# The last 64 tokens of one attention parity laid behind the other, so that two short last units become one full unit

## The chip, the cores and the metric

The kernel runs on one core of a Trainium2 chip. The metric is the device time of one execution in microseconds (us). A time is quoted as the median of several executions. One profiled execution of each kernel gives its trace: the span from first to last event, and for each engine the instructions with start, duration and the event that released them.

Short names in the profile: PE is TensorE (matmuls), PEld its weight loads, DVE is VectorE, ACT is ScalarE, POOL is GpSimd, SP is SyncE, which only issues transfers here. A trailing q (SPq, POOLq) is the engine's instruction sequencer. L562 is line 562 of the kernel file. Matmul lines have other numbers before and after the change, because the file grew.

The runs compared below are in the fast state, with a granted clock (the share of TensorE's full clock that the profile reports) of 0.99 to 1.00.

## The reference, cut to what matters

```python
x = A_x                                    # 1 x 2048 x 512
xn = _layernorm(x)
s = A(xn, wqkv, wo)                        # sliding, dilated attention
g = _silu(B(xn, w1, w2, w3, w4))           # mixer MLP with token shifts
return x + s * g

# A: 32 heads of 16; a token looks at itself and at 7 earlier tokens, 2 apart
W, dil = 8, 2
idx = pos[:, None] - arange(W)[None, :] * dil
logits = where(idx >= 0, q . k[idx] * Dh ** -0.5, -1e9)
o = softmax(logits) . v[idx];  A = o @ wo

# B
h  = gelu(_layernorm(x) @ w1);  hs = shifted quarters of h @ w2
x1 = x + hs
B  = x1 + gelu(_layernorm(x1) @ w3) @ w4
```

The dilation of 2 means that even tokens see only even tokens and odd tokens only odd ones. The kernel therefore works on two parities of M = 1024 tokens each. Inside a parity the window is 8 adjacent tokens.

## The kernel before

A parity is cut into units of queries. A unit of nq queries needs nq + 8 keys, so 120 queries fill the 128 partitions with keys. The first unit has 128 queries (no halo). 1024 = 128 + 7 x 120 + 56, so each parity ends in a short unit of 56 queries:

```python
NQ, M = 120, S // 2
units = [(0, P, 0, P)]                     # (first query, queries, first key, keys)
while units[-1][0] + units[-1][1] < M:
    q0 = units[-1][0] + units[-1][1]
    nq = min(NQ, M - q0)
    units.append((q0, nq, q0 - W, nq + W))
NU = len(units)                            # 9, the last one short
```

Each unit costs the same number of instructions, whatever its length:

```python
def values(p, u):                          # 4 matmuls of 512 columns      (L542)
    ...
    for dt in range(ND):
        nc.tensor.matmul(vp[:nk, :], lhsT=xnT[p][:, dt, k0 : k0 + nk], rhs=wv_sb[:, dt, :], ...)

def scores(p, u, dd):                      # twice per unit: 16 matmuls of nq columns (L562), 2 exps (L567)
    ...
            nc.tensor.matmul(st[:nk, b, i * nq : (i + 1) * nq],
                             lhsT=kT[e][r : r + 32, dt, k0 : k0 + nk],
                             rhs=qT[e][r : r + 32, dt, q0 : q0 + nq], ...)
        nc.scalar.activation(prv[:nk, 2 * h : 2 * h + 2], st[:nk, :, 0 : 4 * nq], AF.Exp, scale=SCALE)

def weighted(p, u, va, prs):               # 32 matmuls of nq columns      (L585)
    ...
```

Between the two score halves of a unit the kernel places matmuls of other work, so that TensorE has something to do while ScalarE computes the exps. In parity 0 this filler is the remaining q/k projections ("q", 4 matmuls, L414) and the w2 tiles ("w", 4 matmuls, L452):

```python
for n, (a, b) in enumerate((("www", "qq"), ("q", "wq"), ("q", "wq"), ("q", "ww"), ("q", "ww"),
                            ("q", "ww"), ("q", "ww"), ("q", "ww"), ("q", "w"))):
    # a: filler after the first score half, b: after the second
```

In parity 1 it is the w4 tiles (11 matmuls each, L516). Between the parities lies w3 (176 matmuls, L496) without attention. After parity 1 come eight more w4 tiles, and beside them the final tiles: attention output times wo (L672), times the gate (VectorE, L680), plus x (VectorE, L682), and the store of the result.

```python
weighted(*prev)()
...
for i in (0, 2, 4):
    store(nc.sync, 0, i)                   # 2 row tiles each
for t in range(8, 16):
    w4s[t](0, NF)
    ...                                    # one final tile beside each w4 tile
```

All long-lived data lies in one large "arena" at fixed offsets; a region is used again when its first owner is done.

The softmax here doesn't subtract the row's maximum and nothing guards it: scores larger than these inputs give would overflow.

## Time and profile before

| | before |
|---|---|
| time, median of 3 runs | 209.36 us (209.29 to 209.38) |
| span of the profiled execution | 207.58 us |
| TensorE busy | 198.6 us, 96% |
| VectorE, ScalarE, GpSimd busy | 66%, 65%, 36% |
| head: start to the first scores of parity 0 | 45.99 us |
| parity 0: to the first w3 matmul | 45.92 us |
| w3: to the first scores of parity 1 | 38.51 us |
| parity 1: to the last weighted sum | 44.39 us |
| last weighted sum to the end of the last w4 matmul | 25.57 us |

From the page of the kernel before: the busy table (engine, busy us, share of the span, number of instructions) and the chain that ended last, by engine.

```profile
PE 198.6 (96%) x1990; PEld 97.0 (47%) x2019; DVE 137.2 (66%) x269; ACT 133.9 (65%) x162; POOL 75.3 (36%) x146
PE 75%; DVE 11%; POOL 6%; issue 3%; ACT 3%; DMA 1%
```

TensorE is the bound.

The end of parity 0 in the TensorE timeline of before (start us, duration us, engine, line, operation, operands, shapes, count):

```profile
...
87.98 0.50 PE L562 MATMUL s_ps<-arena 32*64 32x56 bf16 x16
...
89.82 1.03 PE L542 MATMUL v_ps<-wv_sb,arena 128*128 128x512 bf16 x4
90.77 0.33 PE L562 MATMUL s_ps<-arena 32*64 32x56 bf16 x16
...
91.91 1.89 PE L496 MATMUL w_ps<-arena 128*128 128x512 bf16 x8
93.73 0.39 PE L585 MATMUL o_ps<-arena,v_aug 64*32 64x56 bf16 x32
...
```

The two lines with 32x56 are the scores of the short unit of parity 0. The line L585 with 64x56 is its weighted sum; it is already inside w3, because a weighted sum is always issued behind the next unit's first scores. The last matmul of a group is drawn out to its modelled end, so the cost of a group is best read as the distance to the start of the next one: 16 short scores cost 0.26 to 0.43 us, 32 short weighted matmuls 0.33 us.

The end of parity 1 in the same view:

```profile
...
171.13 0.33 PE L562 MATMUL s_ps<-arena 32*64 32x56 bf16 x16
...
173.36 0.33 PE L562 MATMUL s_ps<-arena 32*64 32x56 bf16 x16
...
174.81 0.39 PE L585 MATMUL o_ps<-arena,v_aug 64*32 64x56 bf16 x32
175.36 2.32 PE L516 MATMUL w_ps<-arena 128*128 128x512 bf16 x10 [0.16 <-issue]
```

```profile
174.36 0.39 PE L585 MATMUL o_ps<-arena,v_aug 64*32 64x56 bf16 x32
174.68 2.55 PE L516 MATMUL w_ps<-arena 128*128 128x512 bf16 x11
```

The stages by windows of time. Columns: window, its length, then busy time and instruction count of PE, PEld, DVE, ACT and POOL, the granted clock, DMA share and GB/s.

```profile
45.99:91.91 45.92, 45.16 (x684) 22.23 (x693) 33.40 (x58) 38.51 (x50) 23.08 (x48) 1.00 0.58 124
91.91:130.42 38.51, 38.30 (x205) 17.74 (x208) 13.68 (x31) 23.16 (x25) 6.85 (x13) 1.00 0.74 164
130.42:174.81 44.39, 43.92 (x680) 21.30 (x688) 30.60 (x39) 37.03 (x46) 15.74 (x22) 1.00 0.42 95
174.81:200.38 25.57, 25.30 (x147) 11.70 (x150) 21.10 (x35) 5.04 (x8) 4.03 (x8) 1.00 0.37 104
```

In each of the four stages TensorE is busy all but a small part, and no other engine comes near it except ScalarE in the two attention stages (38.5 and 37.0 us).

### The profile page before, as it was taken

The numbers are of one execution on the slowest core, as the hardware profiler recorded it, in microseconds if no ns is written. First come the engines' busy times: TensorE is split into PE (matmuls) and PEld (weight loads), VectorE is DVE, ScalarE is ACT, GpSimd is POOL, SyncE is SP. The second block draws the span as 40 slices with busy tenths as digits, with TensorE's granted clock in tenths as the row PEclk, the third lists the DMA queues.
The fourth block names the chain that finished last, engine by engine and source line by source line (L and its number), as shares of the span: only waits on it lengthen the run. The fifth ranks groups of instructions, "written<-read, shape, count | busy, mean of one in ns | idle before, by whom it ended". The sixth has DMA issues, their size and how long they took to land.

```text
span 207.6 us, 4987 instructions
## 1 busy us (share of the span) xinstructions
PE 198.6 (96%) x1990; PEld 97.0 (47%) x2019; DVE 137.2 (66%) x269; ACT 133.9 (65%) x162; POOL 75.3 (36%) x146
## 2 busy tenths in 40 slices
PE   7899999999999999999999999999999999999991
PEld 2565455444544445454444444444445444444440
DVE  4789988645387888787860100268666959779794
ACT  2374878868988888775556555898889875122120
POOL 6788544300032869940164000000850392700000
PEclk9999999999999999999999999999999999999999
DMA  5992066046810576786358994779040042455202
GB/s 145 351 348 71 7 101 96 1 71 101 257 52 0 141 158 107 154 190 113 106 118 216 169 313 92 106 162 305 6 86 3 13 109 42 97 151 156 75 32 101
DMA packets 30575, 25.56 MB, mean 123 GB/s; under 512 B 12488, under 2 KB 28200, under 8 KB 30552
## 3 DMA queue, kind: packets, MB, share of 16 engines
q1 hardware_dynamic: 28360, 21.96, 42.9%
q0 software_dynamic: 2048, 3.15, 9.0%
q8 instruction: 16, 0.26, 0.6%
q10 hardware_dynamic: 144, 0.13, 0.2%
q14 instruction: 7, 0.06, 0.1%
HBM read 12.39 MB, written 4.46 MB: 81 GB/s over the span
## 4 chain that ended last, share of the span: by engine, by line
PE 75%; DVE 11%; POOL 6%; issue 3%; ACT 3%; DMA 1%
PE w_ps L516 19%; PE w_ps L496 18%; PE v_ps L542 8%; PE w_ps L452 7%; PE s_ps L562 6%; PE wo_ps L672 6%; PE o_ps L585 4%; PE qk_ps L414 4%; POOL l1r L273 3%; PE w_ps L429 3%; DVE l1s L280 2%; ACT arena L567 2%; DVE arena L327 1%; DVE l0s L303 1%; DMA arena<-in_A_x_dram 1%
## 5 line engine op out<-in xcount | busy, mean ns | idle before, releaser
L567 ACT ACTIVATE arena<-s_ps 128x960 bf16<-128x960 f32 (+2 forms) x72 | 63.0, 928 | 13.7 <-PE s_ps L562 13.4
L516 PE MATMUL w_ps<-arena 128*128 128x512 bf16 (+1 forms) x156 | 38.5, 380 | 0.5 <-issue 0.2
L501 ACT ACTIVATE arena<-w_ps 128x1024 bf16<-128x1024 f32 x20 | 20.5, 1023 | 15.3 <-PE w_ps L496 14.6
L627 POOL DMA_DIRECT2D arena<-orw x48 | 25.0, 527 | 8.7 <-DVE orw L597 7.4
L496 PEld LDWEIGHTS <-arena 128*128 128x128 bf16 (+1 forms) x176 | 17.6, 100 | 20.2
L516 PEld LDWEIGHTS <-arena 128*128 128x128 bf16 (+1 forms) x176 | 16.4, 98 | 19.6 <-issue 0.4
L546 DVE CAST v_aug<-v_ps 128x512 bf16<-128x512 f32 (+1 forms) x18 | 12.4, 689 | 19.5 <-PE v_ps L542 19.5
L682 POOL TENSOR_TENSOR arena<-arena 128x512 bf16<-128x512 bf16 x6 | 7.7, 1302 | 45.0 <-DVE arena L680 45.0
L531 ACT ACTIVATE sig<-arena 128x512 bf16<-128x512 bf16 x16 | 10.1, 630 | 21.4 <-DVE arena L522 21.4
L597 DVE CAST orw<-o_ps 128x960 bf16<-128x960 f32 (+2 forms) x18 | 19.7, 1094 | 2.1 <-PE o_ps L585 2.1
L496 PE MATMUL w_ps<-arena 128*128 128x512 bf16 (+1 forms) x86 | 19.4, 379 | 0.1
L398 PE MATMUL qk_ps<-arena 128*128 128x512 bf16 (+1 forms) x102 | 18.6, 329 | 0.8 <-ACT arena L320 0.5
L496 PE MATMUL w_ps<-arena,arena 128*128 128x512 bf16 (+1 forms) x86 | 19.1, 379 | 0.1
L542 PE MATMUL v_ps<-wv_sb,arena 128*128 128x512 bf16 (+1 forms) x71 | 18.5, 380 | 0.1
L562 PEld LDWEIGHTS <-arena 32*128 32x128 bf16 (+1 forms) x576 | 10.8, 94 | 15.6 <-issue 15.5
L562 PE MATMUL s_ps<-arena 32*128 32x120 bf16 (+2 forms) x576 | 16.8, 211 | 0.1
L272 POOL TENSOR_SCALAR l3r<-l3m 128x1 f32<-128x1 f32 (+1 forms) x10 | 2.3, 226 | 38.5 <-DVE l3m L281 38.5
L522 DVE TENSOR_TENSOR arena<-w_ps,arena 128x512 bf16<-128x512 f32 x16 | 11.1, 692 | 7.8 <-PE w_ps L516 7.7
L653 DVE TENSOR_TENSOR arena<-arena,orw 128x1440 bf16<-128x1440 bf16 (+1 forms) x2 | 1.7, 842 | 21.3 <-DMA orw<-rden_d 21.3
L452 PE MATMUL w_ps<-arena 128*128 128x512 bf16 x63 | 15.2, 380 | 0.2 <-issue 0.2
L429 PE MATMUL w_ps<-arena 128*128 128x512 bf16 x62 | 14.4, 379 | 0.1
L398 PEld LDWEIGHTS <-arena 128*128 128x128 bf16 x104 | 10.0, 98 | 7.5 <-DMA arena<-in_A_wqkv_dram 0.6
(101 smaller groups left out, 283.9 us busy)
## 6 DMA issues: line engine op xcount, KB each, us to landing
arena<-arena SPq DMA_DIRECT2D x48, 64.0 KB, 2.5
x1n_dram<-arena SPq DMA_DIRECT2D x4, 512.0 KB, 3.4
arena<-in_A_x_dram SPq DMA_DIRECT2D x4, 512.0 KB, 5.2
out_dram<-arena SPq DMA_DIRECT2D x7, 256.0 KB, 2.1
arena<-in_A_x_dram SPq DMA_DIRECT2D x6, 256.0 KB, 7.1
arena<-in_B_w_dram SPq DMA_DIRECT2D x1, 1376.0 KB
arena<-in_B_w_dram SPq DMA_DIRECT2D x1, 1280.0 KB
arena<-in_A_wqkv_dram SPq DMA_DIRECT2D x2, 512.0 KB, 4.5
```

The costliest lines, as they stand in the source:

```text
L398: nc.tensor.matmul(pt[:, b, hh * w : (hh + 1) * w], lhsT=wqk_sb[:, dt, nt * P : (nt + 1) * P], rhs=xnT[p][:, dt, k * CH + hh * w : k * CH ...
L429: nc.tensor.matmul(pt[:, b, :], lhsT=w1_sb[:, dt, g * P : (g + 1) * P], rhs=xn2T[c][:, dt, :], start=(dt == 0), stop=(dt == ND - 1),)
L452: nc.tensor.matmul(pt, lhsT=w2_src(p, g, m0), rhs=w2_sb[:, g, :], start=(g == 0), stop=(g == ND - 1))
L496: nc.tensor.matmul(pt[:fs, ft % 2, :], lhsT=w3_sb[:, dt, ft * P : ft * P + fs], rhs=x1nT[c][:, dt, :], start=(dt == 0), stop=(dt == ND - 1),)
L501: nc.scalar.activation(h3(c, 2 * a, 2), pt, AF.Gelu_apprx_tanh)
L516: nc.tensor.matmul(pt, lhsT=h3(c, ft, 1)[:fs, 0, jj * P : (jj + 1) * P], rhs=w4_sb[:fs, ft, :], start=(ft == 0), stop=(ft == NF - 1),)
L542: nc.tensor.matmul(vp[:nk, :], lhsT=xnT[p][:, dt, k0 : k0 + nk], rhs=wv_sb[:, dt, :], start=(dt == 0), stop=(dt == ND - 1),)
L562: nc.tensor.matmul(st[:nk, b, i * nq : (i + 1) * nq], lhsT=kT[e][r : r + 32, dt, k0 : k0 + nk], rhs=qT[e][r : r + 32, dt, q0 : q0 + nq], s ...
L567: nc.scalar.activation(prv[:nk, 2 * h : 2 * h + 2], st[:nk, :, 0 : 4 * nq], AF.Exp, scale=SCALE)
L597: nc.vector.tensor_copy(out=orw[p][:, :, :, q0 - ra : q0 - ra + nq], in_=op[:, :, 0 : 4 * nq].rearrange("p j (s q) -> p j s q", q=nq),)
L627: nc.gpsimd.dma_start(out=oT[p][DH * hh : DH * (hh + 1), :, ra : ra + rw], in_=orw[p][32 * cg : 32 * cg + DH, jj],)
L672: nc.tensor.matmul(pt, lhsT=oT[p][:, dt, i * P : (i + 1) * P], rhs=wo_sb[:, dt, :], start=(dt == 0), stop=(dt == ND - 1),)
```

## The change

The intent: do not pay for two short units. Parity 0 gets 8 units and stops 56 tokens early. Its last 64 tokens, of which the first 8 are the halo, are laid into columns 1024 to 1087 behind parity 1. Then parity 1's last unit has 56 + 64 = 120 queries, a full unit. (The 8 halo columns also run as queries; their results are thrown away.) The number of units falls from 18 to 17.

The extra columns have to be filled for q, k, the mask rows and the transposed input, and the results of the 56 tokens must come back to parity 0. Because each lengthened buffer of q, k and the transposed input needs 0.5 KB more per partition, the arena map was redone. One ring of buffers went from 3 to 2. And the same filler tiles had to be spread over 8 units of parity 0, not 9. The diff, cut to its core:

```diff
+    DW = 64
     units = [(0, P, 0, P)]
     while units[-1][0] + units[-1][1] < M:
         q0 = units[-1][0] + units[-1][1]
-        nq = min(NQ, M - q0)
-        units.append((q0, nq, q0 - W, nq + W))
+        units.append((q0, NQ, q0 - W, NQ + W))
     NU = len(units)
+    N1 = NU - 1
+    order = [(0, u) for u in range(N1)] + [(1, u) for u in range(NU)]
...
-    fin = ctx.enter_context(tc.tile_pool(name="fin", bufs=3))
+    fin = ctx.enter_context(tc.tile_pool(name="fin", bufs=2))
...
+    X = M + DW
-    arenas = [... enumerate((164, 16))]               # KB
+    arenas = [... enumerate((166 * KB + 160, 16 * KB))]
... (all offsets of the arena map)
 def mask_fill(k):
+                if k:
+                    nc.vector.tensor_copy(out=(kT, qT)[w][e][:, :, M:X], in_=mask[:, w, DW : 2 * DW]...)
...
+    def stage_x():
+        nc.gpsimd.tensor_copy(out=xnT[1][:, :, M:X], in_=xnT[0][:, :, M - DW : M])
...
 def qk_pair(c, a, halves=1):
                 nc.scalar.copy(out=dst[:, n0 : n0 + 2, k * CH : (k + 1) * CH], in_=pt)
+                if c == 1:
+                    nc.scalar.copy(out=dst[:, n0 : n0 + 2, M:X], in_=pt[:, :, CH - DW : CH])
...
 def normalise_end(p, r):          # the columns past M go to parity 0's output
+        if rw > n:
+            a = M - DW + W
+            nc.vector.tensor_tensor(out=oT[0][:, :, a:M], in0=oT[p][:, :, a + DW : X], ...)
...
-        (("www", "qq"), ("q", "wq"), ("q", "wq"), ("q", "ww"), ("q", "ww"), ("q", "ww"), ("q", "ww"), ("q", "ww"), ("q", "w"))
+        (("www", "qq"), ("q", "ww"), ("qw", "qw"), ("q", "ww"), ("qw", "qw"), ("q", "ww"), ("qw", "qw"), ("q", "w"))
...
-                load_w4()
-                load_wo()
+            if c == 1 and a == 0:
+                load_wo()
+                load_w4()
...
+    w4s[8](0, 4)                  # 4 matmuls before the last weighted sum
     weighted(*prev)()
...
-    fq = [(0, 6), (0, 7)] + [(1, i) for i in range(8)]
+    fq = [(0, 6)] + [(1, i) for i in range(6)]
     for t in range(8, 16):
-        w4s[t](0, NF)
+        w4s[t](4 * (t == 8), NF)
...
-    final_tile(1, 5, ps=psa)
-    store(nc.sync, 1, 4)
+    final_tile(0, 7, ps=psa)      # needs the last unit now, so it moved to the end
+    store(nc.sync, 0, 7, 1)
```

The two row tiles (0, 6) and (0, 7) were stored together before; now they end far apart and are stored one by one.

More of the change, by code (lines that the diff above doesn't have):

```diff
@@ L54 @@
         q0 = units[-1][0] + units[-1][1]
-        nq = min(NQ, M - q0)
-        units.append((q0, nq, q0 - W, nq + W))
+        units.append((q0, NQ, q0 - W, NQ + W))
     NU = len(units)
+    N1 = NU - 1
+    order = [(0, u) for u in range(N1)] + [(1, u) for u in range(NU)]
     runs = []
-    for cuts in ((0, 3, 6, NU), (0, 3, 6, NU)):
+    for cuts in ((0, 3, 6, N1), (0, 3, 6, NU)):
         runs.append(
@@ L78 @@
     KB = 512
-    arenas = [const.tile([P, n * KB], BF16, name=f"arena{i}") for i, n in enumerate((164, 16))]
+    X = M + DW
+    arenas = [const.tile([P, n], BF16, name=f"arena{i}") for i, n in enumerate((166 * KB + 160, 16 * KB))]
     def at(kb, n, m):
-        ar, o = (arenas[0], int(kb * KB)) if kb < 164 else (arenas[1], int((kb - 176) * KB))
+        ar, o = (arenas[0], int(kb * KB)) if kb < 170 else (arenas[1], int((kb - 176) * KB))
         return ar[:, o : o + n * m].rearrange("p (n m) -> p n m", n=n)
@@ L85 @@
     xn = [at(8 * p, M // P, D) for p in range(2)]
-    kT = [at(16 + 8 * e, ND, M) for e in range(2)]
-    qT = [at(32 + 8 * e, ND, M) for e in range(2)]
-    kq = [[at(48 + 16 * p + 8 * w, ND, M) for w in range(2)] for p in range(2)]
-    mask = at(152, 2, M)
-    wide = at(157, 2, M)
-    xnT = [at(80 + 8 * p, ND, M) for p in range(2)]
-    hT = [at(96 + 8.5 * p, ND, M + 2) for p in range(2)]
-    wqk_sb = at(113, ND, 2 * D)
-    w1_sb = at(121, ND, D)
-    w2_sb = at(125, ND, D)
-    xn2T = [at(129 + 4 * (c % 2), ND, CH) for c in range(NCH)]
@@ L97 @@
-    w3_sb = at(137, ND, F)
-    prob = [at(148 + 4 * i, 1, H * P // 2) for i in range(4)]
-    orws = [const.tile([P, 2 * ND * RW], BF16, name=f"orw{i}") for i in range(2)]
-    oT = [at(176, ND, M), at(129, ND, M)]
-    xn3 = at(129, TPC, D)
-    x1nT = [at(a, ND, CH) for a in (133, 188, 184, 148)]
-    h3T = [at(a, NF, CH) for a in (48, 96, 107)]
-    h3T_lo, h3T_hi = at(80, 8, CH), at(188, NF - 8, CH)
-    w4_sb = at(118, NF, D)
-    wo_sb = at(59, ND, D)
-    xo = [at(137, M // P, D), at(64, M // P, D)]
@@ L108 @@
-    rr_at = (184, 72)
+    kT = [at(16 + 8.5 * e, ND, X) for e in range(2)]
+    qT = [at(33 + 8.5 * e, ND, X) for e in range(2)]
+    kq = [[at(50 + 8.5 * w, ND, X) for w in range(2)], [at(67 + 8 * w, ND, M) for w in range(2)]]
+    xnT = [at(83, ND, M), at(91, ND, X)]
+    hT = [at(99.5 + 8.03125 * p, ND, M + 2) for p in range(2)]
+    B0 = 115.5625
+    wqk_sb = at(B0, ND, 2 * D)
+    w1_sb = at(B0 + 8, ND, D)
+    w2_sb = at(B0 + 12, ND, D)
+    xn2T = [at(B0 + 16 + 4 * (c % 2), ND, CH) for c in range(NCH)]
@@ new lines @@
+    w3_sb = at(B0 + 24, ND, F)
+    Q0 = B0 + 24 + 10.75
+    prob = [at(Q0 + 4 * i, 1, H * P // 2) for i in range(4)]
+    mask = at(Q0 + 4, 2, M)
+    wide = at(Q0 + 9, 2, M)
+    orws = [const.tile([P, 2 * ND * RW], BF16, name=f"orw{i}") for i in range(2)]
+    oT = [at(176, ND, M), at(B0 + 17, ND, X)]
+    xn3 = at(B0 + 17, TPC, D)
+    x1nT = [at(a, ND, CH) for a in (62, 188, 184, Q0)]
+    h3T = [at(a, NF, CH) for a in (50, 99.5, 110.5)]
+    h3T_lo, h3T_hi = at(83, 8, CH), at(188, NF - 8, CH)
@@ L110 @@
+    w4_sb = at(121.5, NF, D)
+    wo_sb = at(62, ND, D)
+    xo = [at(B0 + 25.5, M // P, D), at(67, M // P, D)]
+    rr_at = (184, 75)
+    sg_at = (61, 66, B0 + 33.5)
     cnt = {"v": 0, "p": 2, "b": 0, "r": 0, "g": 0}
@@ L169 @@
     warm(10)
-    tab = at(148, 3, P + 24)
+    tab = at(Q0, 3, P + 24)
     mg = small.tile([P, 4], F32, name="mg", tag="mg", bufs=1)
@@ L246, in mask_fill @@
                 )
+                if k:
+                    nc.vector.tensor_copy(
+                        out=(kT, qT)[w][e][:, :, M:X],
+                        in_=mask[:, w, DW : 2 * DW].unsqueeze(1).to_broadcast([P, ND, DW]),
+                    )
     def spread(p, lo, hi, q=nc.sync, ws=(0, 1)):
@@ L365, in stage_d @@
         r2 = r2s.pop(c)
-        dg = at(156, TPC, P)
+        dg = at(Q0 + 8, TPC, P)
         for j in range(TPC):
@@ L577, in weighted @@
             rw = runs[p][r][3]
-            orw[p] = orws[(3 * p + r) % 2][:, 0 : 2 * ND * rw].rearrange("p (j s q) -> p j s q", j=2, s=ND)
+            orw[p, r] = orws[(3 * p + r) % 2][:, 0 : 2 * ND * rw].rearrange("p (j s q) -> p j s q", j=2, s=ND)
         op = pst("o", "o_ps")
@@ L597, in weighted_out @@
         nc.vector.tensor_copy(
-            out=orw[p][:, :, :, q0 - ra : q0 - ra + nq],
+            out=orw[p, r][:, :, :, q0 - ra : q0 - ra + nq],
             in_=op[:, :, 0 : 4 * nq].rearrange("p j (s q) -> p j s q", q=nq),
@@ L611, in normalise @@
             out=den_d.rearrange("(j c) x -> c j x", j=2),
-            in_=orw[p][DH : P : 32].rearrange("c j s q -> c j (s q)"),
+            in_=orw[p, r][DH : P : 32].rearrange("c j s q -> c j (s q)"),
         )
@@ L628, in pack @@
                     out=oT[p][DH * hh : DH * (hh + 1), :, ra : ra + rw],
-                    in_=orw[p][32 * cg : 32 * cg + DH, jj],
+                    in_=orw[p, r][32 * cg : 32 * cg + DH, jj],
                 )
@@ L646, in normalise_rr @@
         else:
-            rr = at(rr_at[r % 2] if p else 121, 1, ND * rw)[:, 0, :]
+            rr = at(rr_at[r % 2] if p else B0 + 8, 1, ND * rw)[:, 0, :]
         nc.sync.dma_start(out=rr, in_=rden_d.unsqueeze(1).to_broadcast([8, DH, ND * rw]))
@@ L652, in normalise_end @@
         _, _, ra, rw = runs[p][r]
+        rr = rrs[p, r].rearrange("p (s q) -> p s q", s=ND)
+        n = min(rw, M - ra)
         nc.vector.tensor_tensor(
-            out=oT[p][:, :, ra : ra + rw], in0=oT[p][:, :, ra : ra + rw],
-            in1=rrs[p, r].rearrange("p (s q) -> p s q", s=ND), op=ALU.mult,
-        )
+            out=oT[p][:, :, ra : ra + n], in0=oT[p][:, :, ra : ra + n], in1=rr[:, :, 0:n], op=ALU.mult
+        )
+        if rw > n:
+            a = M - DW + W
+            nc.vector.tensor_tensor(
+                out=oT[0][:, :, a:M], in0=oT[p][:, :, a + DW : X], in1=rr[:, :, a + DW - ra : rw], op=ALU.mult
+            )
     def load_wo():
@@ L676, in final_tile @@
         cnt["g"] += 1
-        sg = at(75 + cnt["g"] % 4, 1, D)[:, 0, :]
+        sg = at(sg_at[cnt["g"] % 3], 1, D)[:, 0, :]
         if act:
@@ L748 @@
         qk_pair(1, a)[0]()
+    stage_x()
     stage_t(2, 0)
@@ L767 @@
     mask_fill(1)
-    spread(0, CH, M)
+    spread(0, CH, X)
     stage_w1(2, 1)
@@ L773 @@
     va = values(0, 0)
-    N1 = NU
-    order = [(p, u) for p in range(2) for u in range(NU)]
-    groups = {n: ([], []) for n in range(2 * NU)}
+    groups = {n: ([], []) for n in range(len(order))}
     def w2_and(t):
@@ L791 @@
     assert not w2q and not qkq
-    late = {n: [] for n in range(2 * NU + 4)}
+    late = {n: [] for n in range(len(order) + 4)}
     def st3(n, *ts):
@@ L800 @@
     late[3] += [lambda: ln3_norm(0), lambda: normalise_dn(0, 0), lambda: ln3_turn(0)]
-    st3(4, 4, 5)
-    st3(5, 6)
-    st3(6, 7)
-    late[7] += [lambda: ln3_norm(1), lambda: normalise_dn(0, 1), lambda: ln3_turn(1)]
+    st3(3, 4)
+    st3(4, 5, 6, 7)
+    late[6] += [lambda: ln3_norm(1), lambda: normalise_dn(0, 1), lambda: ln3_turn(1)]
     w4s = [w4_tile(t) for t in range(S // P)]
@@ L828 @@
             b.append(lambda i=i2: final_tile(0, i, nc.gpsimd))
-    for p in range(2):
-        for r, (_, end, _, _) in enumerate(runs[p]):
-            n = p * NU + end
-            if n + 1 < 2 * NU and not (p == 0 and n >= N1):
-                late[n].append(lambda p=p, r=r: pack(p, r))
-                if p:
-                    late[n].append(lambda p=p, r=r: normalise_dn(p, r))
-                if n < 6 or n > N1:
-                    late[n + 2].append(lambda p=p, r=r: normalise_mid(p, r))
-                    late[n + 2].append(lambda p=p, r=r: normalise_rr(p, r))
-                if p and r == 0:
-                    late[n + 4].append(lambda p=p, r=r: normalise_end(p, r))
-    CUT = CH
+    for n, p, r in ((3, 0, 0), (6, 0, 1), (N1 + 3, 1, 0), (N1 + 6, 1, 1)):
+        if (p, r) != (0, 1):
+            late[n].append(lambda p=p, r=r: pack(p, r))
+        if p:
+            late[n].append(lambda p=p, r=r: normalise_dn(p, r))
+        if (p, r) != (0, 1):
+            late[n + 2].append(lambda p=p, r=r: normalise_mid(p, r))
+            late[n + 2].append(lambda p=p, r=r: normalise_rr(p, r))
+    late[N1 + 7].append(lambda: normalise_end(1, 0))
+    CUT = 480
     for w in range(2):
-        late[4 + w].append(lambda w=w: spread(1, 0, CUT, nc.gpsimd, (w,)))
+        late[3 + w].append(lambda w=w: spread(1, 0, CUT, nc.gpsimd, (w,)))
     prev = None
@@ L882 @@
                 ln3_turn(2)
+                pack(0, 1)
                 normalise_end(0, 0)
@@ L899 @@
         load_xo(0, k)
-    for n in range(N1, 2 * NU):
+    for n in range(N1, len(order)):
         attend(n)
@@ L910 @@
         store(nc.sync, 0, i)
-    fq = [(0, 6), (0, 7)] + [(1, i) for i in range(8)]
+    fq = [(0, 6)] + [(1, i) for i in range(6)]
     for t in range(8, 16):
-        w4s[t](0, NF)
-        if t == 11:
+        w4s[t](4 * (t == 8), NF)
+        if t == 10:
             normalise_end(1, 1)
-        if t == 14:
+        if t == 13:
             normalise_end(1, 2)
@@ L921 @@
             gate(t)
-            if i % 2:
+            if p == 0:
+                store(nc.sync, p, i, 1)
+            elif i % 2:
                 store(nc.sync, p, i - 1)
```

## The prediction

> **What bounds the kernel.** TensorE. The page's busy table has PE at 198.6 of 207.6 us (96%), VectorE 66%, ScalarE 65%; granted clock 1.00 throughout. In the chain of waits PE holds 75%, and from 38.8 to 201 us it is almost only PE. Others matter in the layer-norm head (13 to 39 us, VectorE and GpSimd), in the first attention units (ScalarE exps) and in the last 6 us. So a change pays what it takes from the PE stream, if nothing new waits.
>
> **What goes.** Before, each parity ends in a 56-query unit. After, the two are one 120-query unit of parity 1: 17 units, not 18; 68 matmuls and 68 weight loads fewer. Durations from the chain of waits and the PE timeline:
> - parity 0's short unit: values 0.98, scores 0.43+0.26, weighted 0.32 = 2.0 us;
> - parity 1's: values 0.99, scores 2 x 0.3, weighted 0.32, about 0.3 of gaps where PE waits for the short exps = 2.2 us;
> - a full unit: values 0.86 to 0.97, scores 0.34+0.4, weighted 0.53 = 2.2 us.
> Net 2.0 us less PE. A 512-column matmul steps at 0.215 us (4 in 0.86), which agrees with the Trainium skill, "TensorE: Matmul & The Clock Gate", Back-to-back issue gap (512/2.4 + 2.5 ns): values cost as much for 64 keys as for 128, hence the gain.
>
> **What is added, mostly off the path.** Four ScalarE copies of 128 columns (estimate 0.25 us each: a 3-column copy took 0.16, a 512-column one 0.58) at 23 to 30 us, where ScalarE idles about 0.7 us between copies; one GpSimd copy (estimate 0.6 us) into a 2.3 us gap before 31.1; four VectorE mask copies (estimate 0.8 us together) into a 2.65 us gap after 43.5. I give 0.1 us of lost head. The same 12 q/k and 16 w2 tiles now fill eight units, of 5.05 and 5.95 us of PE against about 4.2 and 4.8 us of ScalarE: PE stays the bound. Parity 1's last exps become 0.92 us each instead of 0.48; four w4 matmuls (0.86 us) are put before their consumer to cover that. I give 0.2 us there and 0.2 us in and around w3.
>
> **Path.** About 1.5 us of the 2.0 reach the end; the tail after the last w4 tile is as before (about 6 us).
>
> **Predicted:** 207.9 us (0.7% less), 8 in 10 within 207.1 to 208.8. Faster by over 2%: 0.02; within 2%: 0.96; slower: 0.02.
>
> **What would show it.** PE busy falls about 2 us; score and weighted groups count 544 instead of 576, values 68 instead of 72. Parity 0's attention, first scores to first w3 matmul, shortens by about 1.8 us; w3 keeps about 38.5 us; parity 1's attention grows by at most 0.5 us, the moved w4 matmuls not counted. Last w4 matmul to end is unchanged.
>
> **What would make it wrong.**
> - The last softmax normalisation is needed one w4 tile (3.24 us) earlier. Its chain (denominator write, reciprocal, broadcast) took about 16.5 us from the last weighted sum; after, VectorE asks for it at about 18. If transfers, now of 360 not 296 queries, are over 2 us slower, VectorE blocks and PE starves: +1 to 2 us.
> - The third w3 chunk's input landed only 1 to 2 us before its use at 111 us; its producer starts about 0.7 us later, beside a pack now moved into w3. A miss stalls PE directly.
> - w4 now loads behind wo, and must land before parity 1 starts, with about 6 us to spare.
> - Units with two q/k tiles may make ScalarE late: +0.1 us each.

## More of the kernel before

The end of the program: the first and last TensorE and VectorE pieces behind the last w4 matmul, from the chain of waits of before (start us, us, what), and then SyncE's wait for transfers behind the last line of the kernel (us in total, times, longest).

```profile
...
200.38 0.88 PE wo_ps L672 x4
...
204.46 0.43 DVE arena L682
```

```profile
...
SPq L959 <- DMA out_dram<-arena: 1.7, 2, 1.0
...
```

The last w4 matmul ends at 200.38, the last VectorE add at 204.89, the span at 207.58. The line with 0.16 us is the last one shown of the end of parity 1 in the TensorE timeline of before.

## The result and the profile after

A ratio below is the mean time of one kernel's fast runs over the mean of the other's fast runs of the same rounds, so it is not quite the ratio of the quoted medians.

| | before | after | difference |
|---|---|---|---|
| time, median | 209.33 us | 208.26 us (208.13 to 208.32) | -1.07; ratio 0.9948 (0.9931 to 0.9965) |
| span of the profiled execution | 207.58 | 206.29 | -1.29 |

The page of the kernel after:

```profile
PE 198.1 (96%) x1951; PEld 95.8 (46%) x1951; DVE 137.6 (67%) x272; ACT 133.9 (65%) x162; POOL 75.8 (37%) x147
PE 75%; DVE 11%; POOL 6%; ACT 3%; issue 2%; DMA 1%
```

68 weight loads are gone (2019 to 1951), as a whole unit of 4 + 32 + 32 should take with it. The busy time seems to have fallen by 0.5 us only. That comparison is not fair: after has a record of every matmul and before lacks 29. A trace of the same matmuls with all 2019 records comes below and has 200.1 us busy, so the fall is 2.0 us.

The end of parity 0 in the TensorE timeline of after. The two short score groups and their values matmuls are gone; w3 starts 2.04 us earlier, and the weighted sum inside w3 is now a full one.

```profile
...
88.37 0.41 PE L578 MATMUL s_ps<-arena 32*128 32x120 bf16 x16
...
89.87 1.89 PE L512 MATMUL w_ps<-arena 128*128 128x512 bf16 x8
91.69 0.60 PE L601 MATMUL o_ps<-arena,v_aug 128*32 128x120 bf16 x32
...
```

The end of parity 1 in the same view. The last unit is a full one, and nine w4 matmuls stand before its weighted sum: five of tile 7, and the four of tile 8 that the change put there.

```profile
171.29 0.47 PE L578 MATMUL s_ps<-arena 32*128 32x120 bf16 x16
171.70 2.12 PE L532 MATMUL w_ps<-arena 128*128 128x512 bf16 x9
173.75 0.61 PE L601 MATMUL o_ps<-arena,v_aug 128*32 128x120 bf16 x32
...
```

The stages by windows, in the same order and columns as before:

```profile
46.04:89.87 43.83, 43.57 (x625) 20.94 (x625) 32.48 (x56) 35.70 (x46) 18.43 (x40) 1.00 0.56 115
89.87:128.59 38.72, 38.72 (x208) 17.89 (x208) 14.36 (x32) 23.75 (x25) 11.27 (x21) 1.00 0.74 181
128.59:173.75 45.16, 45.16 (x693) 21.64 (x693) 30.75 (x41) 38.59 (x47) 15.74 (x22) 1.00 0.40 92
173.75:198.67 24.92, 24.92 (x146) 11.47 (x146) 20.98 (x35) 5.01 (x8) 4.03 (x8) 1.00 0.38 111
```

The end of the program, from the chain of waits and from SyncE's waits:

```profile
...
198.67 0.88 PE wo_ps L694 x4
...
202.75 0.43 DVE arena L704
```

```profile
...
SPq L981 <- DMA out_dram<-arena: 2.3, 1, 2.3
...
```

All together:

| stage | before us | after us | difference |
|---|---|---|---|
| head, to the first scores | 45.99 | 46.04 | +0.05 |
| parity 0, to the first w3 matmul | 45.92 | 43.83 | -2.09 |
| w3, to the first scores of parity 1 | 38.51 | 38.72 | +0.21 |
| parity 1, to the last weighted sum | 44.39 | 45.16 | +0.77 |
| to the end of the last w4 matmul | 25.57 | 24.92 | -0.65 |
| from there to the last VectorE add | 4.51 | 4.51 | 0.00 |
| from there to the end of the span | 2.70 | 3.12 | +0.42 |
| time less span | about 1.8 | about 2.0 | about +0.2 |

Up to the last w4 matmul the change gains 1.71 us. The +0.77 and -0.65 belong together: four w4 matmuls (0.86 us) moved across the border, so the two stages lost 0.12 us together. Then 0.42 us go between the last add and the end of the span, although the work there is the same, and about 0.2 us more outside the span. Two questions were open: why did 0.6 us vanish at an end that does the same work in another order, and is the rest really the merge, or the new arena map and filler order that came with it?

### The profile page after: what moved, and what is told of

Read it like the earlier page. It is cut to its first block, busy times and chain, and to the rows that moved or that the text cites. A ratio compares the mean times of both kernels' runs of the same rounds, so it can differ in the third digit from the quotient of the medians.

```text
span 206.3 us, 4888 instructions
## 1 busy us (share of the span) xinstructions
PE 198.1 (96%) x1951; PEld 95.8 (46%) x1951; DVE 137.6 (67%) x272; ACT 133.9 (65%) x162; POOL 75.8 (37%) x147
## 4 chain that ended last, share of the span: by engine, by line
PE 75%; DVE 11%; POOL 6%; ACT 3%; issue 2%; DMA 1%
PE w_ps L532 19%; PE w_ps L512 19%; PE v_ps L558 7%; PE s_ps L578 6%; PE w_ps L468 6%; PE wo_ps L694 6%; PE o_ps L601 4%; PE qk_ps L430 4%; POOL l1r L284 3%; PE w_ps L445 3%; DVE l1s L291 2%; ACT arena L583 2%; DVE arena L338 1%; DVE l0s L314 1%; DMA arena<-in_A_x_dram 1%
## 5 line engine op out<-in xcount | busy, mean ns | idle before, releaser
L583 ACT ACTIVATE arena<-s_ps 128x960 bf16<-128x960 f32 (+1 forms) x68 | 62.8, 978 | 14.4 <-PE s_ps L578 14.4
L532 PE MATMUL w_ps<-arena 128*128 128x512 bf16 (+1 forms) x164 | 39.1, 380 | 0.0
L517 ACT ACTIVATE arena<-w_ps 128x1024 bf16<-128x1024 f32 x20 | 20.5, 1024 | 14.9 <-PE w_ps L512 14.2
L532 PEld LDWEIGHTS <-arena 128*128 128x128 bf16 (+1 forms) x176 | 16.5, 98 | 19.6
L562 DVE CAST v_aug<-v_ps 128x512 bf16<-128x512 f32 x17 | 11.7, 688 | 14.7 <-PE v_ps L558 14.7
L613 DVE CAST orw<-o_ps 128x960 bf16<-128x960 f32 (+1 forms) x17 | 19.7, 1157 | 2.5 <-PE o_ps L601 2.4
L512 PE MATMUL w_ps<-arena 128*128 128x512 bf16 (+1 forms) x88 | 19.5, 379 | 0.1
L558 PE MATMUL v_ps<-wv_sb,arena 128*128 128x512 bf16 x68 | 17.5, 380 | 0.1
L578 PEld LDWEIGHTS <-arena 32*128 32x128 bf16 x544 | 10.1, 92 | 14.5 <-issue 14.4
L578 PE MATMUL s_ps<-arena 32*128 32x120 bf16 (+1 forms) x544 | 15.8, 214 | 0.0
L468 PE MATMUL w_ps<-arena 128*128 128x512 bf16 x64 | 15.7, 380 | 0.1
L445 PE MATMUL w_ps<-arena 128*128 128x512 bf16 x64 | 14.6, 379 | 0.0
```

The lines of the kernel that those rows point to most:

```text
L445: nc.tensor.matmul(pt[:, b, :], lhsT=w1_sb[:, dt, g * P : (g + 1) * P], rhs=xn2T[c][:, dt, :], start=(dt == 0), stop=(dt == ND - 1),)
L468: nc.tensor.matmul(pt, lhsT=w2_src(p, g, m0), rhs=w2_sb[:, g, :], start=(g == 0), stop=(g == ND - 1))
L512: nc.tensor.matmul(pt[:fs, ft % 2, :], lhsT=w3_sb[:, dt, ft * P : ft * P + fs], rhs=x1nT[c][:, dt, :], start=(dt == 0), stop=(dt == ND - 1),)
L517: nc.scalar.activation(h3(c, 2 * a, 2), pt, AF.Gelu_apprx_tanh)
L532: nc.tensor.matmul(pt, lhsT=h3(c, ft, 1)[:fs, 0, jj * P : (jj + 1) * P], rhs=w4_sb[:fs, ft, :], start=(ft == 0), stop=(ft == NF - 1),)
L578: nc.tensor.matmul(st[:nk, b, i * nq : (i + 1) * nq], lhsT=kT[e][r : r + 32, dt, k0 : k0 + nk], rhs=qT[e][r : r + 32, dt, q0 : q0 + nq], s ...
```

## The experiments

Twelve runs were made, all with correct results (control repeats the changed kernel, and before_mem and before_mem5 are one kernel). Each was timed beside runs of the kernel before on the same chip.

### control: the changed kernel once more

No edit.

> The changed kernel again, unedited, as the yardstick for the other runs of this call. Expected 208.2 to 208.35 us. It also tells whether the difference between a run's time and its profiled span (1.74 us in the one profiled run of before, 1.90 to 2.02 us in four of after) is steady.

Measured: 208.32 us (208.10 to 209.11, six runs), ratio 0.9951 (0.9939 to 0.9964). The result repeats. One of six runs was 0.8 us longer; its span was longer as well.

### after_120 and before_121: the number of transfers

The theory: at its end the program waits on SyncE for the transfers still out, one semaphore after another, eight of them in a fixed order. The transfers use these eight in turn. Before issues 120 of them (counted in the program; the trace records 108), so the last store uses the eighth semaphore, the one waited for last. After issues 121 (109 recorded), so the last store uses the first; SyncE stands at it until the store has landed, and then still has to go through the seven others. The rival: the last final tile or its store is itself slower in after, because the order of the tail was changed.

after_120 takes one transfer away from after and changes nothing else:

```diff
-    for i in (0, 2, 4):
-        store(nc.sync, 0, i)
+    store(nc.sync, 0, 0, 4)
+    store(nc.sync, 0, 4)
```

> The changed kernel with two of its output stores made one, so that it issues 120 hardware-queue transfers as the kernel before did, not 121. Theory A (the end of the program waits for eight transfer semaphores one after the other in fixed order; with 121 transfers the last store sits on the first of them, so seven more waits of about 60 ns follow it): 0.4 us less than control, and the stretch from the last VectorE instruction to the span's end returns from 3.12 to about 2.7 us. Rival B (the longer end is the last stores' own landing, or chance of one run): no change, within 0.1 us of control.

before_121 adds one to before:

```diff
-    for i in (0, 2, 4):
-        store(nc.sync, 0, i)
+    store(nc.sync, 0, 0)
+    store(nc.sync, 0, 2)
+    store(nc.sync, 0, 4, 1)
+    store(nc.sync, 0, 5, 1)
```

> The kernel before with one output store cut in two, so 121 transfers. Theory A: 0.4 us slower than before, about 209.75 us, the stretch after the last VectorE instruction growing from 2.7 to about 3.1 us. Rival B: as before, within 0.1 us.

Measured: after_120 207.89 us, ratio 0.9925 (0.9913 to 0.9937), 0.43 us less than the control. before_121 209.77 us, ratio 1.0016 (1.0004 to 1.0028), 0.33 us more than before. SyncE's waits at the end, first of after_120 and then of before_121:

```profile
...
SPq L981 <- DMA out_dram<-arena: 1.7, 2, 1.0
...
```

```profile
...
SPq L961 <- DMA out_dram<-arena: 2.3, 1, 2.3
...
```

after_120 now reads exactly as before did (two waits, 1.7 us), and before_121 as after did (one wait of 2.3 us). From the last packet of the last store to the end of the span before took 1.27 us and after_120 1.26; after took 1.69 and before_121 1.68. The difference of 0.42 us over seven further waits is about 0.06 us each. The packed traces hold the waits themselves: in after SyncE's wait for the first of the eight semaphores ends when the last store has landed, at 204.97 us, and the seven others follow about 0.06 us apart, the last at 205.39; in before the wait for the eighth ends at 206.68 and none follows. The theory stands and the rival falls: one transfer more or less, issued long before the end, moves the end by 0.3 to 0.4 us.

### after_split: the merge undone, everything else kept

The last full unit is cut into its two parts of 56 and 64 queries. Arena map, filler order, extra copies and the tail stay.

```diff
     NU = len(units)      # moved down
+    q0 = units.pop()[0]
+    for s0, nq in ((q0, M - q0), (M, DW)):
+        units.append((s0, nq, s0 - W, nq + W))
...
-    N1 = NU - 1
+    N1 = NU - 2
... (the 11 matmuls of w4 tile 7 spread 3, 3, 5 over the two units)
```

> The changed kernel with only the merged unit taken apart again: its last unit of parity 1 becomes one of 56 queries and one of 64, everything else (memory map, group order, loads, tail) stays. Theory A (the whole gain is one unit's work less on TensorE): about 1.9 us slower than control, near 210.1 us, with values, scores and weighted groups back at 72, 576 and 576. Rival C (part of the gain comes from the new group order in parity 0 or from the new tail): clearly less than 1.9 us slower, the rest of the gain staying.

Measured: 210.63 us, ratio 1.0053 (1.0040 to 1.0066): 2.3 us more than the control. The end of parity 1 in the TensorE timeline shows where it stands still:

```profile
...
174.48 0.35 PE L581 MATMUL s_ps<-arena 32*72 32x64 bf16 x16
175.33 1.02 PE L535 MATMUL w_ps<-arena 128*128 128x512 bf16 x4 [0.50 <-DVE arena L541]
...
```

0.5 us of the 2.3 is this wait for VectorE, which the way in which I spread the filler made. The other 1.8 us, found by subtraction, are the work of one more short unit. So the merge alone is worth about 1.8 us, more than the whole of the gain: the rest of the change costs.

### after_nofill: the four moved w4 matmuls put back

```diff
-    w4s[8](0, 4)
     weighted(*prev)()
...
-        w4s[t](4 * (t == 8), NF)
+        w4s[t](0, NF)
```

> The changed kernel with the four w4 matmuls that were put before the last weighted sum put back after it (the same work, only the order changes). Theory A (the merged unit's last two exps of 0.92 us end about 2.3 us after its second score set begins, and TensorE has only 0.35+1.08 us of other work for that time): TensorE idles about 0.8 us before the last weighted sum, and the kernel is 0.6 to 0.8 us slower than control, near 209.0 us. Rival D (the filler hides nothing; the tail has slack for it): within 0.1 us of control.

Measured: 208.71 us, ratio 0.9967 (0.9955 to 0.9980), 0.3 us (by the ratios) to 0.4 us (by the medians) more than the control. The weighted sum in the TensorE timeline:

```profile
172.95 0.50 PE L601 MATMUL o_ps<-arena,v_aug 128*32 128x120 bf16 x24
173.72 0.29 PE L601 MATMUL o_ps<-arena,v_aug 128*32 128x120 bf16 x8 [0.27 <-ACT arena L583]
```

The stall is there, but smaller than I expected. I had reckoned with the whole weighted sum waiting for the last exp. Only its last 8 matmuls read what that exp writes; 24 of 32 run before it. The move is worth its line, about 0.3 to 0.4 us.

### after_regroup: another filler order in parity 0

The chain of waits of after has ScalarE on it just where parity 0 turns into w3:

```profile
...
88.44 0.43 PE s_ps L578 x16
88.86 0.97 ACT arena L583
89.83 0.04 issue
89.87 1.89 PE w_ps L512 x8
...
```

The last unit has only one w2 tile behind its second scores ("q", "w"), and then w3 has to wait until an exp has emptied its PSUM bank (a part of the memory that TensorE writes its results to). A second place is the third unit ("qw", "qw"): its first half brings a q/k copy on ScalarE that the values of the next unit wait for, 0.23 us. The edit, on top of after_120, moves one w2 tile from the first place to the other end:

```diff
-        (("www", "qq"), ("q", "ww"), ("qw", "qw"), ("q", "ww"), ("qw", "qw"), ("q", "ww"), ("qw", "qw"), ("q", "w"))
+        (("www", "qq"), ("q", "ww"), ("q", "qw"), ("q", "ww"), ("qw", "qw"), ("q", "ww"), ("qw", "qw"), ("q", "ww"))
```

> 120 transfers, and one w2 tile moved from parity 0's third unit to its last. Theory A (the changed kernel's trace shows TensorE waiting about 0.2 us in the third unit for a PSUM bank that a late ScalarE copy holds, and 0.2 us at the switch to w3 for a bank that the last exps hold): 0.2 to 0.4 us less than after_120, near 207.6 us, parity 0's attention (first scores to first w3 matmul) falling from 43.83 to about 43.5 us. Rival F (the waits only move to other units): within 0.1 us of after_120.

Measured: 207.39 us (207.28 to 207.46), ratio 0.9902 (0.9887 to 0.9917), 0.50 us less than after_120, a little more than the 0.2 to 0.4 us expected. The same place in its chain:

```profile
...
87.41 0.34 PE s_ps L578 x16
87.75 1.83 PE w_ps L468 x8
89.59 1.73 PE w_ps L512 x8
...
```

No ScalarE between scores and w3 any more. Parity 0 takes 43.32 us instead of 43.83; w3 (38.72) and parity 1 (45.17) are as in after. So 0.5 us of the merge's gain had been given back by the filler order that the change chose. This is the best version that was found: 1.0% under before, 0.4% under after.

### best: an add moved to GpSimd, and why the name is wrong

On top of after_120, the final add of tile (0, 7) goes to GpSimd, to shorten VectorE's string at the end, which is on the chain (0.42 us):

```diff
-    final_tile(0, 7, ps=psa)
+    final_tile(0, 7, nc.gpsimd, ps=psa)
```

> 120 transfers, and the closing add of the output tile that comes third from last moved from VectorE to GpSimd. Theory A (after TensorE's last output tile the end is a serial string of VectorE instructions, so one of 0.42 us less ends it 0.42 us earlier): 0.4 us less than after_120, near 207.5 us; the stretch from the last w4 matmul to the span's end, 7.2 us in after_120, becomes 6.8. Rival E (the end is set by the stores, or GpSimd slows VectorE): no gain.

Measured: 210.03 us, ratio 1.0032 (1.0019 to 1.0045): 2.1 us more than after_120, where 0.4 less was expected. A plain miss, for two reasons. First, VectorE in the timeline of best, and GpSimd beside it:

```profile
...
201.07 1.10 DVE L702 TENSOR_TENSOR arena<-arena 128x512 bf16<-128x512 bf16 x1 [0.19 <-ACT arena L701]
...
```

```profile
200.37 1.53 POOL L704 TENSOR_TENSOR arena<-arena 128x512 bf16<-128x512 bf16 x1 [20.45 <-DVE arena L702]
```

The multiply of tile (1, 6) took 1.10 us instead of 0.42 while the GpSimd add ran, and ended 0.27 us behind it. The Trainium skill, "SBUF — State Buffer", SBUF: two separate sides, says that VectorE and GpSimd share a pair of ports by an exclusive lock and the loser blocks for the whole instruction; it names a VectorE operation with two SBUF inputs beside a GpSimd operation that reads SBUF, which is the case here. This one pair of instructions agrees: the multiply began at 201.07, inside the add (200.37 to 201.90).

Second, and larger, the last instructions of GpSimd's sequencer. The first line is of best, the second of after_120 (count, shortest, median and longest ns, first and last start):

```profile
...
L981 POOLq DRAIN  x3: 40/102/6888, 200.3 to 207.7; - x3
...
```

```profile
...
L981 POOLq DRAIN  x3: 40/102/6503, 179.3 to 205.7; - x3
...
```

GpSimd ends the program with a DRAIN of 6.5 to 6.9 us. In after_120 it begins at 179.3, beside GpSimd's last transfer issue, is over at 185.8, and nobody sees it. In best it begins at 200.3, together with the add, ends at 207.2, and all engines wait for it at the last barrier: from the last packet to the end of the span 2.88 us instead of 1.26.

### best2: best and after_regroup together

> All three: 120 transfers, the add on GpSimd, the w2 tile moved. If the three are independent, as theory A has it, near 207.2 us, 1.1 us less than control and 2.2 us less than before. If not, no better than the better one of best and after_regroup.

Measured: 209.63 us, ratio 1.0009 (0.9997 to 1.0022): 0.4 us less than best and 2.2 us more than after_regroup. The two edits add up; the filler order's half microsecond does not depend on the tail.

### best3 and best4: the last tiles in another order

On top of after_regroup, best3 puts the final tile (0, 7) before the last w4 tile:

```diff
             final_tile(p, i, ps=psa)
+            if t == 14:
+                final_tile(0, 7, ps=psa)
+                store(nc.sync, 0, 7, 1)
             gate(t)
...
-    final_tile(0, 7, ps=psa)
-    store(nc.sync, 0, 7, 1)
     gate(15)
```

> after_regroup with the output tile that came third from last put before the last w4 tile instead of after it (nothing goes to GpSimd). Theory A (from the last w4 matmul to the end TensorE does not bound the kernel but a string of VectorE instructions of 3.6 us does, a third of it for that tile; put earlier, it fits in VectorE's idle time beside the last w4 tile's matmuls): TensorE's last w4 matmul ends 0.86 us later, the stretch from it to the span's end falls from 7.2 to about 5.7 us, and the kernel gains about 0.6 us, near 206.8 us. Rival G (VectorE is full there as well and only hands the delay on): within 0.1 us of after_regroup.

Measured: 207.66 us (one of six runs 208.62), ratio 0.9925 (0.9909 to 0.9942), 0.3 us (by the medians) to 0.5 us (by the ratios, which include the 208.62) more than after_regroup, where 0.6 less was expected. One run of before took 509.27 us; it is left out. Taking work from VectorE behind the last w4 tile did not help, because VectorE then stands and waits for the gate's tanh:

```profile
...
200.51 0.69 DVE L548 SCALAR_TENSOR_TENSOR arena<-sig,arena 128x512 bf16<-128x512 bf16 x1 [0.76 <-ACT sig L547]
...
```

best4 fills this wait with tile (1, 6), straight from PSUM without the copy by ScalarE:

```diff
-    gate(15)
-    final_tile(1, 6, ps=psa, act=True)
+    final_tile(1, 6, ps=psa)
     store(nc.sync, 1, 6, 1)
+    gate(15)
```

> best3 with the last tile but one, (1,6), finished before the last gate, straight from PSUM, in place of after it by way of a ScalarE copy. Theory J (best3's trace shows VectorE idle for 0.76 us while the last gate's tanh runs, then a string of 2.6 us: gate, (1,6), (1,7); with (1,6) in the idle time the string after the tanh is 0.6 + 0.6 + 0.4): 0.4 to 0.5 us less than best3, near 207.2 us. Rival K (stores or something else hold the end): as best3, 207.66 us.

Measured: 207.48 us, ratio 0.9909 (0.9894 to 0.9924): the same as after_regroup within the intervals. The multiply from PSUM takes 0.69 us where the one from the copy took 0.42. These two edits found no slack in the tail and are not worth having.

### before_mem and before_mem5: the kernel before with after's memory sizes

After pays for a larger arena and one buffer less. Is that dear, and does it explain the roughly 0.2 us outside the span? The edit of before: same offsets and same instructions, only the sizes of after. (The two kernels are the same; the first was one look, the second was timed in five rounds.)

```diff
-    fin = ctx.enter_context(tc.tile_pool(name="fin", bufs=3))
+    fin = ctx.enter_context(tc.tile_pool(name="fin", bufs=2))
...
-    arenas = [... (164, 16)]
+    arenas = [... (166.3125, 16)]
```

> The kernel before with nothing but the sizes of its on-chip buffers set to those of the changed kernel (arena 166.3 KB, two output buffers instead of three). It looks for one thing, the time outside the profiled span: 1.76 us in kernels made from before, 1.94 to 2.03 in those made from after. If the memory map makes the difference it shows about 1.95 here; if something else of the program does, 1.76.

> before_mem again, timed: its one run was 208.86 us where before had 209.39, though TensorE, VectorE and GpSimd run the same instructions; its trace lacks a stall of 0.3 us that before has at 60.6 us, where ScalarE starts an exp 0.36 us after its scores are ready with nothing in the way that the profile shows. Theory H (such stalls belong to the built program and not to one run; part of the changed kernel's gain is that it happens not to have this one): 208.8 to 208.9 us in every run, ratio to before about 0.9975. Rival I (one run's chance): 209.3 to 209.4 us.

Measured: before_mem 208.86 us (one run, state unknown); before_mem5 208.92 us (208.88 to 208.93), ratio 0.9978 (0.9965 to 0.9990). The sizes do not cost, the kernel gets 0.5 us faster. It does the same matmuls as before, and its trace has all 2019 records:

```profile
PE 200.1 (97%) x2019; PEld 96.9 (47%) x2019; DVE 137.3 (66%) x269; ACT 133.9 (65%) x162; POOL 75.1 (36%) x146
```

A piece of the half microsecond can be seen in the chain of waits, first before and then before_mem5:

```profile
...
60.19 0.43 PE s_ps L562 x16
60.62 0.29 issue
60.91 0.04 ACT arena L567
...
```

```profile
...
60.20 0.34 PE s_ps L562 x16
60.54 0.97 PE w_ps L452 x4
...
```

In before, ScalarE's exp begins at 60.91 although the scores it waits for were done at 60.55; in before_mem5 the same exp begins at 60.62. The 0.29 us stay: parity 0 takes 45.63 us instead of 45.92. Another 0.16 us are gone in parity 1 (44.23 instead of 44.39), where before has a second such exp: it begins at 154.77, 0.35 us after its wait ended, and in before_mem5 only 0.06 us after. Both traces have the same instructions on TensorE, VectorE, GpSimd and SyncE; ScalarE's stream differs only in a few semaphore waits. Which of the two sizes moves them was not separated.

The traces hold a hint. In before an 8 KB packet of an instruction queue (q14) starts 0.67 us after each of the two late exps begins, at 61.58 and 155.44. In before_mem5 the first of these packets (61.63) comes 0.67 us behind a ScalarE semaphore wait instead; this wait is late (60.95, 0.34 us after the exp in front of it, where most such waits follow within 0.03 us) and delays nothing. In after the same is seen at 152.92. So it looks as if one ScalarE instruction is late by about 0.3 us at such a place, and the instructions in front of it decide whether that is an exp. No run tests this, and the cause stays open. What is shown is that about 0.45 us of the distance between before and after belongs to a property of the built program before, and not to the merge.

The time outside the span did not move with the sizes: 1.79 us in before_mem, 1.76 in before.

## Why the prediction was right or wrong

The time was right: 207.9 predicted, 208.26 measured, inside the range of 207.1 to 208.8. But 0.36 us are missing, and the sum behind it had two terms that are absent and some errors that cancel. Now that the parts are measured, the difference of -1.07 us can be made up from them. The merge's rows, except for the head, compare before_mem5 with after_regroup, which are free of the late exp and of the filler loss.

| part | us | from |
|---|---|---|
| merge, parity 0 | -2.31 | 45.63 to 43.32 |
| merge, head | +0.05 | first scores, before to after |
| merge, w3 | +0.22 | 38.50 to 38.72 |
| merge, parity 1 and w4 tiles behind it | +0.28 | 69.80 to 70.08 |
| filler order | +0.51 | parity 0, 43.32 to 43.83 |
| late exps of before, not in after | -0.45 | before to before_mem5, up to the last w4 matmul |
| semaphore order at the end | +0.42 | last add to end of span |
| outside the span | about +0.2 | time less span |
| sum | about -1.1 | measured -1.07 |

Point by point, in the order of the prediction:

- **TensorE bounds the kernel: right.** In after its busy time fills each of the last three windows to the hundredth. (Waits under about 0.16 us behind a group cannot be seen so: the last matmul of a group is listed with 0.38 us, against a step of 0.215.)
- **Gross 2.0 us of TensorE work: right.** With all records, busy time falls from 200.1 to 198.1 us. Where the time lies was right as well: parity 0 loses the short unit's values 0.98, scores 0.69, and a full weighted sum (0.53) that slips into w3, together 2.2 us; measured 2.09, and 2.31 once the filler order is repaired. (The prediction's own figure for parity 0 was about 1.8.) The estimate was built on a step of 0.215 us for a matmul of 512 columns, and the traces keep it throughout.
- **0.3 us of gaps in parity 1's short unit: wrong.** I read the 0.16 us "issue" lines as TensorE waiting for short exps. They were missing records; before_mem5 has all records and no gap there. So a full unit costs parity 1 about 0.3 us more than a short one, where I had set the two equal.
- **0.2 us for parity 1's last exps: the size right, the reason not.** With the moved w4 matmuls no exp is waited for at all. What is lost is that 0.3 us of work: 0.28 us against before_mem5, and 0.12 against before, which loses 0.16 of its own there. Without the move 0.3 to 0.4 us more would be lost (after_nofill).
- **0.1 us of lost head: right**, 0.05 measured.
- **0.2 us in and around w3: right by accident.** w3's own +0.21 is the full weighted sum that moved into it, which the sum above has already counted as leaving parity 0.
- **"TensorE stays the bound" in the eight units, with ScalarE's total of 4.2 to 4.8 us against 5.05 to 5.95: too coarse.** I compared totals of a unit. What counted was the order inside it: at the third unit and at the turn to w3, TensorE waited for one particular ScalarE result. That is +0.51 us, which the text named only as a risk of 0.1 us for each unit with two q/k tiles.
- **Stream gain 1.5 us, measured 1.71: right by luck.** Without the late exps of before, which I did not see, it would have been 1.26.
- **"The tail after the last w4 tile is as before": this is the step that failed.** It went from 7.20 to 7.62 us. All instructions up to the last add keep their distances (4.51 us both times). The rest is the order of the final semaphore waits, which I did not look at, because the 121st transfer seemed free. after_120 and before_121 show it both ways.
- **The other three risks that I named did not come, one of them narrowly.** The data of the last normalisation had landed at 192.05 us (the last update of its semaphore) and VectorE's wait for it stood at 192.53, 0.5 us to spare, where the prediction spoke of some 1.5 (18 against 16.5 us). In after_regroup nothing was to spare: landed at 192.44, the wait over at 192.47. The third w3 chunk and the later w4 load held nothing up: TensorE has no idle time in those windows.
- **About 0.2 us outside the span: not predicted and not explained.** In the profiled runs the time less the span is 1.76 to 1.79 us in before, before_121, before_mem and before_mem5, 1.91 to 2.03 in the kernels built on after, and 2.11 and 2.14 in best and best2. It is steady to about 0.1 us for one built program. It does not come from the sizes (before_mem) nor from the number of transfers (after_120, before_121). The cause stays open.

The busy times carry one more warning. The Trainium skill, "Perfetto Trace Analysis", Tensor Engine Instruction (MATMUL, LD_WEIGHTS), says that TensorE's ends are estimated by the profiler, not observed. The traces here agree: single matmuls of 512 columns are listed with 380 ns while they start every 215. So this document goes by starts and complete counts, and not by ends.

## What to carry to other kernels

When a unit costs the same number of instructions at any length, merging two short ones saves nearly one whole unit: here 1.8 us of work for some copies that found idle engines. But such a change moves everything around it, so recheck three things that no instruction's duration tells: whether the filler still stands where a single result is awaited, which transfer the program's end waits for last, and whether an engine with a long end of its own (GpSimd here) gets work late. And before reading small gaps in a busy engine, compare the number of records with the number of instructions.

## What the Trainium skill lacked or had wrong

- "Runtime: NRT & Kernel Launch", The ~15µs preamble/postamble breakdown, has a row for the barrier behind the kernel but nothing on the transfers' semaphores: they are waited for one by one in a fixed order, so one transfer more in the whole program moved the end by 0.3 to 0.4 us (after_120 -0.43, before_121 +0.33), about 0.06 us for each wait.
- "VectorE: DVE Perf Modes", The DRAIN you can't avoid, gives the DRAINs that the runtime puts around a kernel as a constant 12 ns or so on all engines. It has nothing on those at the last line of the program itself: GpSimd's took 6.5 to 6.9 us here (after_120, best), and when GpSimd worked late (best) all engines waited for it, 1.6 us of the 2.1 us lost.
- "TensorE: Matmul & The Clock Gate", Back-to-back issue gap, differs from the measurement: it gives about 131 ns for each matmul of 512 columns in a sustained stream of weight loads and matmuls, and 216 ns for an isolated one. Here the sustained stream runs at the isolated figure: 8 matmuls in 1.73 us at the start of w3 (after_regroup), and 176 in about 38.2 us over all of it (after, less the weighted sum), 0.217 us each. The measurement decides.
- No page speaks of the same instructions running half a microsecond faster in another built program: 209.40 against 208.92 us for before and before_mem5, with a ScalarE exp that begins 0.29 us later in the first.
- No page that I found says that the time outside the profiled span depends on the program: 1.79 us in before_mem against 2.11 in best.
